# Two residual additions and a half moved onto TensorE at the end of four attention layers, one last store in place of two, and a new instruction order

## The chip, the cores and the metric

The kernel runs on one core of one Trainium2 chip. The metric is device time in microseconds (us) for one execution, taken as the median of several runs. The engines of the core are named as the profile names them: PE is TensorE (matrix products; PEld is its weight load), DVE is VectorE, ACT is ScalarE, POOL is GpSimd, SP is SyncE, which here only issues DMAs.

## The reference

One sequence of 2048 rows and 512 columns passes through four layers, each with layernorm in front and a residual around it:

```python
x = x + _A_ref(_layernorm(x), A_wqkv, A_wo)   # layer 1: linear attention
x = x + _B_ref(_layernorm(x), B_wqkv, B_wo)   # layer 2: sliding window of 256
x = x + _A_ref(_layernorm(x), A_wqkv, A_wo)   # layer 3, weights as layer 1
x = x + _B_ref(_layernorm(x), B_wqkv, B_wo)   # layer 4, weights as layer 2
```

Both kinds have 32 heads of 16. `_A_ref` maps queries and keys by phi (t + 1 above zero, exp(t) below), sums keys by values over the whole sequence and divides by a sum. `_B_ref` takes a masked softmax over the last 256 rows. Both end in a product with the 512 x 512 matrix `wo`; what comes out of it is added to x. The change touches that addition, in layer 4 alone.

## The kernel before, in words

Rows are worked in 16 tiles of 128. The residual stream x stays on the chip as `xres[:, t, :]`, in bfloat16. Layers are fused across the sequence: keys of layer 1, then its outputs with layer 2 tile by tile, then a barrier (layer 3 needs the sum over all tiles), then layer 3's outputs with layer 4.

A tile of layer 4 goes as follows. Scores are products on PE (L676, at the window's far edge L792 and L745), exponents of them on ACT (L686, L801, L754), masks on DVE (L694, L773) or POOL (L772). The products of weights and values run on PE (L822); DVE takes reciprocals (L834) and divides (L835) into `o`. `o` is transposed, by a DMA on SP (L389) or for the last tiles by PE with an identity (L395, L860) and a copy out (L402, L407). Then `tok` (L409 to L423) makes four products of 512 columns with `wBo` into one PSUM bank, in two groups of two (L420). `resid` (L602) lets DVE add the bank and `xres` into `xres` (L604, called `res`), and a store of 128 KB, `outp` (L942), goes out on POOL's or SP's queue.

The last tile has a function of its own, `b_last` (L849). It transposes and multiplies in halves as they become ready: a group of two products of 512 columns (L871), then two groups of two products of 256 columns. Two DVE additions of 256 columns follow (L877), each with a store of 64 KB on SP (L878).

`WHOLE` (L218) names tiles whose residual is to be added on PE, by a product of `ident` and `xres` into the same bank. It is empty for both layers, so that code lies idle.

Nothing is scheduled at run time. `Graph.add` collects operations with their readers and writers. All operations that touch one PSUM tile are chained: each depends on the one before it on that tile (`deps.add(last)`), whatever its columns. `place` unpacks `TABLE`, which holds for each operation its place in one overall order, its engine where it may have two (copies: ACT or DVE; far masks `mf`: DVE or POOL; `outp`: POOL or SP), and the PSUM bank of each tile. Each engine then plays its own operations strictly in that order and waits on semaphores where an input comes from another. A DMA waits in SP's line until its input is ready, and what stands behind it waits too.

The functions that the diff touches:

Of the kernel before, what the change touches and what calls it, by code (L numbers as in the profile page):

```python
# [9 lines left out]
ALU = mybir.AluOpType  # L10
# [207 lines left out]
WHOLE = {2: (), 3: ()}  # L218
# [17 lines left out]
class Plan:  # L236
# [173 lines left out]
    def tok(self, name, t, lhs, rhs, rd, key, whole=False):  # L410

        K = self
        ps = Tile(1, K.cls)
        if whole:
            self.pe("id", lambda e: e.matmul(K.ps(ps), K.ident[:], K.xres[:, t, :], start=True, stop=False), key - 0.01, 1, 512, rd=[("xres", t), ("ident",)], ps=[ps])
        for h in range(2):
            def put(e, h=h):
                m = None
                for c in (2 * h, 2 * h + 1):
                    m = e.matmul(K.ps(ps), lhs(c), rhs(c), start=c == 0 and not whole, stop=c == 3)  # L420
                return m
            self.pe(name, put, key - 0.001 * h, 2, 512, rd=rd, ps=[ps])
        return ps  # L423
# [170 lines left out]
    def a_out(self, t, key, whole):  # L594
        K = self
        x = lambda f: K.XQ[:, f, t * P:(t + 1) * P]
        po = self.tok("aout", t, x, lambda f: K.M[:, f, :], [("XQ", t)] + [("M", f) for f in range(4)], key + 0.1, whole)
        if whole:
            return po
        self.resid(t, po, key + 0.15)  # L600

    def resid(self, t, po, key):  # L602
        K = self
        self.on("DVE", "res", lambda e: e.tensor_tensor(K.xres[:, t, :], K.ps(po), K.xres[:, t, :], ALU.add), key, dve(512), rd=[("xres", t)], wr=[("xres", t)], ps=[po])  # L604
# [235 lines left out]
    def b_out(self, j, key, by_pe, whole=False):  # L840
        K = self
        s = j % 2
        self.transpose("oT", lambda: K.o[:, s, :], lambda: K.oT[:, s, :, :], [("o", s, 0), ("o", s, 1)], [("oT", s)], key - 0.15, by_pe)
        po = self.tok("bout", j, lambda f: K.oT[:, s, f, :], lambda f: K.wBo[:, f, :], [("oT", s), ("wBo",)], key, whole)
        if whole:
            return po
        self.resid(j, po, key + 0.05)

    def b_last(self, j, key):  # L849
# [4 lines left out]
        for h in range(2):  # L854
# [10 lines left out]
            for n in range(2) if h else [None]:  # L865
                cs = slice(0, D) if n is None else slice(256 * n, 256 * n + 256)

                def put(e, h=h, cs=cs):
                    m = None
                    for f in (h, h + 2):  # L870
                        m = e.matmul(K.ps(po)[:, cs], K.oT[:, s, f, :], K.wBo[:, f, cs], start=f == 0, stop=f == 3, skip_group_check=True)  # L871
                    return m

                self.pe("bout", put, key + 0.1 * h + 0.01 * (n or 0), 2, cs.stop - cs.start, rd=[("oT", s, h), ("wBo",)], ps=[po])
        for n in range(2):
            cs = slice(256 * n, 256 * n + 256)
            self.on("DVE", "res", lambda e, cs=cs: e.tensor_tensor(K.xres[:, j, cs], K.ps(po)[:, cs], K.xres[:, j, cs], ALU.add), key + 0.2 + 0.1 * n, dve(256), rd=[("xres", j)], wr=[("xres", j, n)], ps=[po])  # L877
            self.on("SP", "out", lambda e, cs=cs: e.dma_start(K.out[0, j * P:(j + 1) * P, cs], K.xres[:, j, cs]), key + 0.3 + 0.1 * n, (520, 2400), rd=[("xres", j, n)])  # L878
# [5 lines left out]
    def middle(self, ph):  # L884
# [14 lines left out]
        def front(t):  # L899
            k = base + t  # L900
            po = self.a_out(t, k - par["k_ao"], t in WHOLE[ph])
# [53 lines left out]
    r"c-qZZ1GH_+j;*AUO4YS(+qP}nwr$(CZQHhO+h*^z&%Lkz@5lf8{~o>0SxP0TnVDHN_6n(#3ZYPu0>vt{(khG!tBeY#;;UdPxccG}D67J&gzBTqtRkpSE~5J8",  # L955
    r"5~(cegG;Qksun7VilmaNY^tS-tg@?Cs*n2YqNp6IwMwQYsGKUfimLi5QE62hl|uDX(NtR%N~Ke|RXdeZEmn<GdevXmRuk0{HA!Vqb<_a0O)XUeRbACyrBahs",
    r"V>L)^R~^(cHAU4^JJeJaL)BLuRT{NZEmtvBF_lrRP@U9ZwM)fPomF&oOYK&%RYR3Y4N<q%3Ds5IQA1TX6;}mT2I8o@s=Lag;;Cuso@$~}tCMP&y050IH|msX",
    r"sv4-_YKA(kR;rn5l{%y5s#)r+TCEDIE=r(>daH`7HEN#9t0F*8wMPX~7J8`>s)SmrMk)ur)hP8&1%ml1BJ5SURA4BhvcMd*PmNZIV1b&g_N(_QE38usRV4VJ",
    r"&Zz_HqlygYRdrPi8o&khKqZDKkOYduLv>L_g>2AFtyh=SBb84bRF72<$PQ0bP$&VHRSpOSC84>>2~X7+6&yaPr0`jdQ)5*rIHbO)WY7?j!&emzzNxAzI$Tj9",
    r"pftpQ{OXyC2?}CC1(ge&8n1Fg5S0Q7sXUMp@<J#`1^J+`Dg$L9HGEfPRT>xvjUXhHgE$aW6;S0N9aMnvPyi}H5!D!KLu_aYwP2A-3sqEps0c+>JE#FQVS}ou",  # L960
    r"+Cv?v3-zF!st+BY2^?0Pp@wP$9iauZg;vlKHmWYr3|hkx)d`wIcX+Ojs;{mGOn|O%OihI2YLlw0UZ_d1SzT2x)k4^!CPO8)2(GCq&<&=-3D~L@!*$gYrol;=",
    r"4mZ>$SOV45W>^X{;1mEXgPCwsAuNZvumUvnf_bnKN~&2<Ud@Lsa2RT-*{}e%!V#DQ+n_g`hNG|@*1{{*57xnP*a0_TJ?w;4&<A$GYUm5MU=5rBf{?fYUaPZk",
# [12 lines left out]
    r"RJx;kQv`}eS*Q;kr0BGr`cg!iK!<3Co<uWs49ZH8C??gUi8Poh(=1(!Vo_BBj!nC1IK`noRGW~i&=}G@g6a_QI2uWNX)GP3$<&W_P+b~D_2?M&r=2vOM$=tg",
    r"pL)`9x~CgZFN#aMs5;%(4XGNPq$zZYrqXG;N{4A0ouGI$ovzanvh4U81?50Imx6J8x<MD|3^k(56r3AV0y;~VC?TDrCUk{D@p-yQO(`^Apk{Q7!f-ea$+u}9",
    r"-J$S2pO_a=1b#%(I4m1pNYObbhu~bih=gPCVrovgc?K<^7POyc(qn2#`{)VHqL>_upHd=<&57w5wdFXxl<razT1K;}9p9%p^qgOC5WYtzxIG8vlN^y>aw3kz",
    r"uQ&<E<>wTcU-Jt}%**K%zoZrPfTD0zF2pM-9v9(N6rW$wYD&t5IUncc1iXe4@@vY^YbhB&q>H?cPICdy!=?BVC+9MJhA;CKF3knG92e!Qe3mP4F}}vdxjc8{",
    r"68wg{b45<UCAlp3;7**9yKp5=#g(};r{=d@g$Hp}e#alFC)eh|Tv@;8H2i_9=(Ie9KT%gs$5nMd?!`lS0Dq?5+@I6)0?xp1=q)YeMO=*+b4NbMHFzMO=MLP5",
    r"`|>cZ&cnGT&*2eVhv)G~uFDsAE|21GT#M`Rcb?B{*qL=)pVx9Aqf7%{!RxspFJUmN7|lvv%8j@&2R5U5H8<gRG=`UPP_u!@@<txV8F>?D;_<whC-6sJ&YAf-",  # L980
    r"Pvjux22bKGJejlcR(?;}ISU6fH+dVkHrx3V@8DbfnQ!w>Zpt}$3h(0Ge24Gy9&W~ac`AS5544Z(aaL~5t@u9g=V{!UAMkW;!!7tBx8wtSlxOfUKFG&;CLiKi",
    r"e3&2cY(Bz|`3ZmJr~Hhy$!qc$GQ|v=BBr=0V2YZ2Cb%hR#N;<6j4_2wX%oVfG+|9)Q_6%hWlUMq)>sqXv@_*QdDG9dHxW!s6U&4&9ZX~s%5*dpOn=kKgf>x3",
    r"L^HrlFrCeE)5Q!lUCl((%?vV;%nCEugfYF$BooyPF%`{F6U}rtlT91b+r&0g%p$YW^fANCRMW#$GQ-VcGtKlhqs?@)#Pl>{%qla(EHh(GWfRAYFssc>Q_YMw",
    r"Ys^Sf#mq9}Om#ELR5i0rTvNleGWSd^Gshe?_f1W6+(eVL=7EVW$ILpj*Tj(ZX0F+19-4WkoWzv<W~n)2qMPzE-<&l&%p+4l7MPvpu{mcJnlEOTd1Bt1Z|14_",
    r"U}BhOW`l_(73HgmEeFj<v(dznJ?5~fZQ_~TCa%Oco6I4T*nBdTB#Egk@g#vcVy>8^riwf_2~8q%&1^PX%z1ObTs1GuEA!H9HA<41<bsmiY%>?kMRUV!H?Ivy",
    r"3b|xHo6F{ed1F$Fm6OIv9dpW@Ht{8p)HOFv5J@24O)yDow4{=BCZPlsl6QvXtx0dvNN}kyM$$<JlSo7|n#7V;s!AA1BGsgUgp*sQq1-lMCA9>W406YWkn1L+",
# [182 lines left out]
```

## Time and profile before

| what | us |
|---|---|
| median of 3 runs | 412.12 |
| lowest and highest run | 411.43 and 413.2 |
| the profiled execution, its own time | 412.6 |
| its span, first to last instruction | 410.8 |
| PE busy in the span | 386.9 |
| ACT busy | 352.8 |
| DVE busy | 344.5 |
| POOL busy | 122.4 |

The profiled execution lies 0.48 above the median, and 1.8 of its time lies outside the span. A line such as L604 is a line of the kernel's file. "x4" counts instructions. An entry in square brackets is the time in which the engine sat idle ahead of that instruction, and what ended the wait. A landing time runs from the issue of a DMA to its completion. The timeline merges neighbours on one line, so a row of x2 spans both.

### The profile page before, as it was taken

How to read it: one execution, taken by the hardware profiler on the slowest of the kernel's cores; microseconds unless marked ns; L12 is line 12 of the kernel's file. 1: busy time of each engine (PE TensorE's matmuls, PEld its weight loads, DVE VectorE, ACT ScalarE, POOL GpSimd, SP SyncE). 2: the span in 40 equal slices, each digit the busy share in tenths (PEclk: the TensorE clock that was granted, in tenths of full speed). 3: DMA queues.
4: the chain of work that ended last, by engine and by line, in shares of the span. 5: the costliest groups of instructions: out<-in, count | busy, mean ns of one | idle time of the engine just before them, and what ended most of it. 6: DMA issues, size and time to landing. Idle time of an engine off the chain costs nothing.

```text
span 410.8 us, 17540 instructions
## 1 busy us (share of the span) xinstructions
PE 386.9 (94%) x7668; PEld 260.3 (63%) x7742; DVE 344.5 (84%) x807; ACT 352.8 (86%) x448; POOL 122.4 (30%) x216
## 2 busy tenths in 40 slices
PE   7999999999999999999999999999999988999896
PEld 3654676766575576566567777586757755566674
DVE  6997799989998899888887789997899688857585
ACT  4654659998999999999998357999999999999993
POOL 4576653111252331320503203303113304303020
PEclk9999999999999999999999999999999999999999
DMA  7495114443243435353222100344314821561751
GB/s 249 101 217 144 49 34 115 120 70 90 56 106 74 119 77 107 81 119 82 68 41 57 27 2 2 105 109 81 102 44 122 122 66 41 120 127 56 168 107 42
DMA packets 66596, 37.19 MB, mean 91 GB/s; under 512 B 47640, under 2 KB 61848, under 8 KB 66520
## 3 DMA queue, kind: packets, MB, share of 16 engines
q1 hardware_dynamic: 66032, 34.75, 37.0%
q8 instruction: 61, 1.00, 1.1%
q0 software_dynamic: 480, 1.31, 1.0%
q14 instruction: 15, 0.12, 0.1%
q10 hardware_dynamic: 8, 0.00, 0.0%
HBM read 6.29 MB, written 2.10 MB: 20 GB/s over the span
## 4 chain that ended last, share of the span: by engine, by line
PE 51%; ACT 34%; DVE 9%; DMA 3%; issue 2%; SPq 1%; POOL 1%
ACT pb L686 20%; PE ps L420 18%; PE ps L434 10%; PE ps L822 10%; PE ps L676 5%; ACT pb L801 5%; ACT vp L686 4%; PE ps L501 3%; ACT tE L444 2%; DMA wA<-in_A_wqkv_dram 2%; DMA xT<-xn 1%; DVE xres L604 1%; DVE stats L374 1%; ACT pb L721 1%; PE ps L477 1%
## 5 line engine op out<-in xcount | busy, mean ns | idle before, releaser
L686 ACT ACTIVATE pb<-ps 128x1024 bf16<-128x1024 f32 (+2 forms) x216 | 198.9, 1020 | 5.2 <-PE ps L676 3.9
L822 PEld LDWEIGHTS ps<-vB,pb 128*128 128x128 bf16 x2560 | 77.7, 96 | 12.3 <-DVE pb L694 3.6
L822 PE MATMUL ps<-vB,pb 128*128 128x34 bf16 x2560 | 83.5, 177 | 0.6 <-POOL pb L772 0.3
L434 PE MATMUL ps<-xT,wBp 128*128 128x128 bf16 x1024 | 69.0, 219 | 1.7 <-ACT tE L444 0.6
L434 PEld LDWEIGHTS ps<-xT,wBp 128*128 128x128 bf16 x1024 | 58.5, 98 | 13.7 <-issue 4.4
L379 POOL TENSOR_SCALAR ve<-mv 128x1 f32<-128x1 f32 x63 | 16.7, 265 | 154.7 <-DVE mv L375 152.7
L444 ACT ACTIVATE tE<-ps 128x512 bf16<-128x512 f32 x64 | 38.6, 612 | 27.1 <-PE ps L420 11.2
L772 POOL TENSOR_SCALAR_AFFINE_SELECT pb<-pb 128x1024 bf16<-128x1024 bf16 x30 | 34.4, 1146 | 71.4 <-DVE pb L694 23.8
L676 PE MATMUL ps<-XQ,kB 32*128 32x256 bf16 (+3 forms) x992 | 48.0, 267 | 3.3 <-ACT pb L754 0.7
L604 DVE TENSOR_TENSOR xres<-ps,xres 128x512 bf16<-128x512 f32 x63 | 43.0, 684 | 6.7 <-PE ps L420 6.3
L420 PE MATMUL ps<-wA,XQ 128*128 128x512 bf16 x174 | 45.6, 379 | 2.2 <-issue 0.6
L374 DVE BATCH_NORM_STATS2 stats<-xres 128x6 f32<-128x512 bf16 x64 | 43.5, 685 | 2.8 <-DMA xres<-in_A_x_dram 2.2
L694 DVE TENSOR_TENSOR pb<-pb,tri 128x512 bf16<-128x512 bf16 (+1 forms) x108 | 41.5, 396 | 3.3 <-ACT pb L686 3.1
L801 ACT ACTIVATE pb<-ps 128x1024 bf16<-128x1024 f32 x42 | 41.4, 1059 | 1.1 <-PE ps L792 0.9
L380 POOL TENSOR_TENSOR rs<-ve,negh 128x1 f32<-128x1 f32 x64 | 37.8, 591 | 8.3 <-DVE ve L377 3.0
L434 PE MATMUL ps<-XQ,wA 128*128 128x128 bf16 x512 | 35.4, 219 | 0.3 <-DMA wA<-in_A_wqkv_dram 0.3
L434 PEld LDWEIGHTS ps<-XQ,wA 128*128 128x128 bf16 x512 | 30.7, 98 | 7.3 <-DMA wA<-in_A_wqkv_dram 0.8
L420 PE MATMUL ps<-wBv,xT 128*128 128x512 bf16 x110 | 31.4, 380 | 2.6 <-issue 1.0
L676 PEld LDWEIGHTS ps<-XQ,kB 32*128 32x128 bf16 x992 | 15.0, 92 | 29.5 <-ACT pb L686 7.5
L420 PE MATMUL ps<-M,XQ 128*128 128x512 bf16 x113 | 30.7, 380 | 2.3 <-ACT vp L686 0.4
L420 PE MATMUL ps<-wBo,oT 128*128 128x512 bf16 x105 | 28.8, 380 | 2.8 <-issue 1.0
L686 ACT ACTIVATE vp<-ps 128x1024 bf16<-128x1024 f32 (+2 forms) x32 | 26.7, 928 | 1.5 <-PE ps L676 1.5
(126 smaller groups left out, 551.6 us busy)
## 6 DMA issues: line engine op xcount, KB each, us to landing
vB<-vS SPq DMA_DIRECT2D x64, 136.0 KB, 2.7
kB<-vp SPq DMA_DIRECT2D x60, 128.0 KB, 2.3
wA<-in_A_wqkv_dram SPq DMA_DIRECT2D x3, 512.0 KB, 5.5
out_dram<-xres POOLq DMA_DIRECT2D x10, 128.0 KB, 2.8
xres<-in_A_x_dram SPq DMA_DIRECT2D x2, 512.0 KB, 5.1
pb<-in_B_wqkv_dram SPq DMA_DIRECT2D x1, 1024.0 KB, 5.8
xres<-in_A_x_dram SPq DMA_DIRECT2D x3, 256.0 KB, 5.5
out_dram<-xres SPq DMA_DIRECT2D x5, 128.0 KB, 2.7
```

The costliest lines, as they stand in the source:

```text
L374: self.on("DVE", "stats", lambda e: e.bn_stats(K.stats[:, t, :], x()), key, dve(512), rd=rd, wr=[("stats", t)], **held)
L380: self.pow = self.on("POOL", "pow", lambda e: e.tensor_tensor(K.rs[:, t, :], K.ve[:, t, :], K.negh[:], ALU.pow), key + 0.03, (640, 690), r ...
L420: m = e.matmul(K.ps(ps), lhs(c), rhs(c), start=c == 0 and not whole, stop=c == 3)
L434: m = e.matmul(K.ps(ps)[:, f * P:(f + 1) * P], w(c, f), xT(c), start=c == 0, stop=c == 3)
L444: self.on("ACT", "E", lambda e: e.activation(K.tE[:, s, :], K.ps(ps), ACT.Exp, bias=0.0), key, act(512), wr=[("tE", s)], ps=[ps])
L604: self.on("DVE", "res", lambda e: e.tensor_tensor(K.xres[:, t, :], K.ps(po), K.xres[:, t, :], ALU.add), key, dve(512), rd=[("xres", t)], w ...
L676: m = e.matmul(K.ps(ps[gq])[:, ns * i:ns * i + ns], K.kB[rows, j % 4, 2 * f + b, :, :], K.XQ[rows, f, q:q + ns], start=True, stop=True, ti ...
L686: return e.activation(out(2 * h, 2, ns), i, ACT.Exp, bias=0.0, scale=0.25)
L694: return e.tensor_tensor(x, x, K.tri[:, 0, sh:64].unsqueeze(1).unsqueeze(1).to_broadcast([P, 4, n, 64 - sh]), ALU.mult)
L772: return e.affine_select(out=x, in_=x, compare_op=ALU.is_ge, fill=0.0, base=-2, pattern=[[0, 16], [-2, 64]], channel_multiplier=1)
L801: return e.activation(far(h), i, ACT.Exp, bias=0.0, scale=0.25)
L822: m = e.matmul(K.ps(ps)[:, 34 * u:34 * u + 34], K.P((b // 2) % rp)[:, gq, f, o:o + P], K.vB[:, (b // 2) % 4, b % 2, r, :], start=i == 0, s ...
```

## The change

For tiles 13 and 14 of layer 4 a fifth product, identity by `xres`, closes the group in `tok`. The bank then holds the finished sum, and a copy (`rs`, on ACT or DVE) replaces the addition on DVE. For tile 15 the same is done for columns 256 to 511 alone: an identity product of 256 columns joins the first group; DVE adds columns 0 to 255 and a copy moves the rest. One store of 128 KB replaces the two of 64 KB and depends on both. `a_out` loses the argument `whole`, which it was never given as true.

```diff
-WHOLE = {2: (), 3: ()}
+WHOLE = {2: (), 3: (13, 14)}
...
-        if whole:
-            self.pe("id", lambda e: e.matmul(K.ps(ps), K.ident[:], K.xres[:, t, :], start=True, stop=False), key - 0.01, 1, 512, rd=[("xres", t), ("ident",)], ps=[ps])
         for h in range(2):
             def put(e, h=h):
                 m = None
                 for c in (2 * h, 2 * h + 1):
-                    m = e.matmul(K.ps(ps), lhs(c), rhs(c), start=c == 0 and not whole, stop=c == 3)
+                    m = e.matmul(K.ps(ps), lhs(c), rhs(c), start=c == 0, stop=c == 3 and not whole)
+                if whole and h:
+                    m = e.matmul(K.ps(ps), K.ident[:], K.xres[:, t, :], start=False, stop=True)
                 return m
...
+    def resid(self, t, po, key, whole=False):
+        K = self
         if whole:
-            return po
...
+            self.copy("rs", po, lambda: K.xres[:, t, :], lambda: K.ps(po), key, 512, wr=[("xres", t)])
+            return
...
                     for f in (h, h + 2):
                         m = e.matmul(K.ps(po)[:, cs], K.oT[:, s, f, :], K.wBo[:, f, cs], start=f == 0, stop=f == 3, skip_group_check=True)
+                    if not h:
+                        m = e.matmul(K.ps(po)[:, 256:512], K.ident[:], K.xres[:, j, 256:512], start=False, stop=False, skip_group_check=True)
...
-        for n in range(2):
-            cs = slice(256 * n, 256 * n + 256)
-            self.on("DVE", "res", lambda e, cs=cs: e.tensor_tensor(K.xres[:, j, cs], K.ps(po)[:, cs], K.xres[:, j, cs], ALU.add), key + 0.2 + 0.1 * n, dve(256), rd=[("xres", j)], wr=[("xres", j, n)], ps=[po])
-            self.on("SP", "out", lambda e, cs=cs: e.dma_start(K.out[0, j * P:(j + 1) * P, cs], K.xres[:, j, cs]), key + 0.3 + 0.1 * n, (520, 2400), rd=[("xres", j, n)])
...
+        self.on("DVE", "res", lambda e: e.tensor_tensor(K.xres[:, j, 0:256], K.ps(po)[:, 0:256], K.xres[:, j, 0:256], ALU.add), key + 0.2, dve(256), rd=[("xres", j)], wr=[("xres", j, 0)], ps=[po])
+        self.copy("rs", po, lambda: K.xres[:, j, 256:512], lambda: K.ps(po)[:, 256:512], key + 0.3, 256, rd=[("xres", j)], wr=[("xres", j, 1)])
+        self.on("SP", "out", lambda e: e.dma_start(K.out[0, j * P:(j + 1) * P, :], K.xres[:, j, :]), key + 0.4, (520, 2400), rd=[("xres", j, 0), ("xres", j, 1)])
```

`TABLE` is new as a whole. Unpacked and laid beside the old one it holds 2558 operations for 2559, and differs over the entire kernel, not at its end alone:

- Of the groups of PE 727 of 866 keep their relative order; of ACT's operations 394 of the 437 that it has in both tables, of DVE's 523 of 781, of SP's 137 of 225, of POOL's 135 of 197. In layers 2 to 4 most moves on PE and ACT are swaps of neighbours.
- 52 operations change engines: 24 far masks (14 to POOL, 10 to DVE), 7 `outp` (5 to SP, 2 to POOL), 21 copies (three of them in the place of DVE's additions). 346 of 1005 PSUM tiles get another bank.
- At the end: the copies of tiles 13 and 14 and the half of tile 15 stand on ACT; the copy that empties tile 15's second pair of transposes goes from ACT to DVE; tile 14's last products stand around, not behind, the first transposes of tile 15.
- At the start SP's order was x loads, transposes of tiles 5, 6, 7, a weight load of 1 MB (`wBn`), more transposes, and `wAv` (512 KB) after them all. It becomes transposes of tile 5, `wAv`, tile 6, `wAo` (512 KB), tile 7, `wBn`, the other transposes.
- Around the start of layer 4, ACT hands DVE the copies `bke` of tiles 1, 3 and 4 and the copy of one transposed tile (`Te`); DVE hands ACT `bve` of tiles 0 and 3, `bqe` of tile 4 and one copy `sc`.

More of the change, by code (lines that the diff above doesn't have):

```diff
@@ L419, in put @@
                 for c in (2 * h, 2 * h + 1):
-                    m = e.matmul(K.ps(ps), lhs(c), rhs(c), start=c == 0 and not whole, stop=c == 3)
-                return m
-            self.pe(name, put, key - 0.001 * h, 2, 512, rd=rd, ps=[ps])
+                    m = e.matmul(K.ps(ps), lhs(c), rhs(c), start=c == 0, stop=c == 3 and not whole)
+                if whole and h:
+                    m = e.matmul(K.ps(ps), K.ident[:], K.xres[:, t, :], start=False, stop=True)
+                return m
+            if whole and h:
+                self.pe(name + "i", put, key - 0.001 * h, 3, 512, rd=rd + [("xres", t), ("ident",)], ps=[ps])
+            else:
+                self.pe(name, put, key - 0.001 * h, 2, 512, rd=rd, ps=[ps])
         return ps
@@ L591, in barrier, with a_out @@
                 self.on("DVE", "pqd", lambda e, x=x, b=bc[tg]: e.tensor_tensor(x(), K.ps(b).rearrange("p (f n) -> p f n", f=4), x(), ALU.mult), k + 0.3 + 0.01 * tg, dve(512), rd=[("XQ", t)], wr=[("XQ", t)], ps=[bc[tg]])
-    def a_out(self, t, key, whole):
+    def a_out(self, t, key):
         K = self
         x = lambda f: K.XQ[:, f, t * P:(t + 1) * P]
-        po = self.tok("aout", t, x, lambda f: K.M[:, f, :], [("XQ", t)] + [("M", f) for f in range(4)], key + 0.1, whole)
+        po = self.tok("aout", t, x, lambda f: K.M[:, f, :], [("XQ", t)] + [("M", f) for f in range(4)], key + 0.1)
+        self.resid(t, po, key + 0.15)
+    def resid(self, t, po, key, whole=False):
+        K = self
         if whole:
-            return po
-        self.resid(t, po, key + 0.15)
-    def resid(self, t, po, key):
-        K = self
+            self.copy("rs", po, lambda: K.xres[:, t, :], lambda: K.ps(po), key, 512, wr=[("xres", t)])
+            return
         self.on("DVE", "res", lambda e: e.tensor_tensor(K.xres[:, t, :], K.ps(po), K.xres[:, t, :], ALU.add), key, dve(512), rd=[("xres", t)], wr=[("xres", t)], ps=[po])
@@ L871, in put @@
                         m = e.matmul(K.ps(po)[:, cs], K.oT[:, s, f, :], K.wBo[:, f, cs], start=f == 0, stop=f == 3, skip_group_check=True)
-                    return m
-                self.pe("bout", put, key + 0.1 * h + 0.01 * (n or 0), 2, cs.stop - cs.start, rd=[("oT", s, h), ("wBo",)], ps=[po])
-        for n in range(2):
-            cs = slice(256 * n, 256 * n + 256)
-            self.on("DVE", "res", lambda e, cs=cs: e.tensor_tensor(K.xres[:, j, cs], K.ps(po)[:, cs], K.xres[:, j, cs], ALU.add), key + 0.2 + 0.1 * n, dve(256), rd=[("xres", j)], wr=[("xres", j, n)], ps=[po])
-            self.on("SP", "out", lambda e, cs=cs: e.dma_start(K.out[0, j * P:(j + 1) * P, cs], K.xres[:, j, cs]), key + 0.3 + 0.1 * n, (520, 2400), rd=[("xres", j, n)])
+                    if not h:
+                        m = e.matmul(K.ps(po)[:, 256:512], K.ident[:], K.xres[:, j, 256:512], start=False, stop=False, skip_group_check=True)
+                    return m
+                if h:
+                    self.pe("bout", put, key + 0.1 * h + 0.01 * (n or 0), 2, cs.stop - cs.start, rd=[("oT", s, h), ("wBo",)], ps=[po])
+                else:
+                    self.pe("boutj", put, key, 3, 512, rd=[("oT", s, h), ("wBo",), ("xres", j), ("ident",)], ps=[po])
+        self.on("DVE", "res", lambda e: e.tensor_tensor(K.xres[:, j, 0:256], K.ps(po)[:, 0:256], K.xres[:, j, 0:256], ALU.add), key + 0.2, dve(256), rd=[("xres", j)], wr=[("xres", j, 0)], ps=[po])
+        self.copy("rs", po, lambda: K.xres[:, j, 256:512], lambda: K.ps(po)[:, 256:512], key + 0.3, 256, rd=[("xres", j)], wr=[("xres", j, 1)])
+        self.on("SP", "out", lambda e: e.dma_start(K.out[0, j * P:(j + 1) * P, :], K.xres[:, j, :]), key + 0.4, (520, 2400), rd=[("xres", j, 0), ("xres", j, 1)])
     def phase(self, ph):
@@ L959 @@
[L959 to L962, printed above, removed]
@@ L1007 @@
[L1007 to L1008 removed]
+    r"c-qZa1Gp?nvd#=;=Cy6xwr$(CZQHhO+qP}n=IiP+cXxINJ2P+geJ}fTR%K+wAAg|ot3JV$QlS*65Q>ymtU@bPVN_TZUx^B*tV*Cls_-hI%B()R;Oc{Gp(3b6",
+    r">b=XNBC1cWrOK)jt0XFt%BGU4Rw}!StR|>rs<n!ua;xNOqH3cisT?Y*N}<}SKFX-Hs-2pwVyZl9ipr__s>N!mN~ij%yegL3rfRF$YKd|xn(D8<x<+cLO0Nc}",
+    r"#ww1AtCp$lDy6EUim6m;hZ?Brs`hHR+NnCI3@V;lp^B?+YLMEc>Z$JPmg=aYt0t<x8mt1TPHKocp?0fjYN)!c66xuxsY<OntH7#(%BW_j7;2cxq`Ih?s)x#=",
@@ L1009 @@
+    r"jkW*hfJf5@<k4b-J{2#k+Dl7-Yx0zo=h)u^UP}aU_c`;FwfK4>pi?-Yxc)48I)**66p#deeLXA)$b~Nk-`8Ji@CxXe2egH+2mP7$Lj?30`x;&Q+l~C>JqSN>",
+    r"e@lAi9tS@OKan3!Rlo|A@yhEDQhW@&i@)q%oBX4c{=|DB`8&nu$vewDCjmv{fQQA4Un#G&-kSKQ`e}c0wFmD{pFa=khb?++f6AV>={NK}kt}{<<W1g|0gWQs",
+    r"_h8fi0Kou42m",
 )
```

104 lines of the change are left out of this document (50 added, 54 removed).

## The prediction

> **What bounds the kernel now.** I read the share of each engine on the page, then busy time by stretches, then the chain of work and the timelines of the last 12 us. The stretches:
>
> ```profile
> 9.79:44.00 34.21, 33.47 (x295) 18.98 (x304) 29.33 (x81) 17.91 (x32) 22.34 (x47) 1.00 0.62 156
> 60.00:247.00 187.00, 179.24 (x3604) 121.44 (x3642) 163.42 (x379) 168.40 (x208) 48.15 (x80) 1.00 0.35 79
> 247.00:259.00 12.00, 11.84 (x191) 8.99 (x193) 11.83 (x29) 9.87 (x19) 4.98 (x10) 1.00 0.12 36
> 259.00:292.00 33.00, 32.22 (x647) 22.63 (x652) 29.27 (x67) 33.00 (x39) 7.41 (x12) 1.00 0.38 86
> 292.00:324.00 32.00, 30.50 (x707) 21.45 (x708) 27.90 (x65) 31.52 (x36) 8.85 (x13) 1.00 0.48 97
> 324.00:395.00 71.00, 64.46 (x1708) 44.20 (x1716) 52.07 (x122) 69.62 (x82) 14.00 (x22) 1.00 0.44 97
> 395.00:407.20 12.20, 11.79 (x270) 7.84 (x270) 8.45 (x22) 8.40 (x16) 2.89 (x4) 1.00 0.33 81
> ```
>
> Columns are the stretch, its length, busy time of PE, PEld, DVE, ACT and POOL (instructions in brackets), the granted clock, the DMA share and GB/s. Layer 1 (9.79 to 44) is PE's: 33.47 of 34.21. PE and DVE share 247 to 259. ACT holds 259 to 395, with 1.86 idle of 136. In the 12 us before the closing additions PE is the full one again (11.79 of 12.20), while DVE and ACT work 70% of the time. The granted clock is 1.00 throughout. So DVE, which the change relieves, is not what the end waits for. The chain says it piece by piece (start, length, piece):
>
> ```profile
> 401.26 0.81 PE ps L420 x3
> ...
> 405.14 0.81 PE ps L420 x3
> 405.95 0.11 PE ps L860 x2
> 406.06 0.43 PE ps L871 x2
> 406.50 0.04 issue
> 406.54 0.62 PE ps L871 x4
> 407.16 0.02 issue
> 407.19 0.44 DVE xres L877
> 407.62 0.02 issue
> 407.65 0.42 DVE xres L877
> ```
>
> At 401.26 and 405.14 stand tile 13's and tile 14's products with `wBo`, behind each of which the change puts a fifth. At 406.06 and 406.54 stand tile 15's. DVE enters only at 407.19.
>
> **The change part by part: the end.** (a) Identity products. Four products of 512 columns without a gap took 0.86, one 0.215:
>
> ```profile
> 14.02 0.86 PE ps L501 x4
> ```
>
> Two of 512 columns and one of 256 (half, by columns) make 0.22 + 0.22 + 0.11 = 0.55, and they stand on the chain. Only a wait of PE could cover them, and the chain above shows none over 0.04; that one, ahead of 406.54, goes. That a transpose now stands between tile 14's products changes no sum. I take 0.5; the bounds are 0 (waits hide all) and 0.55.
>
> (b) The additions of tiles 13 and 14 leave DVE, copies come to ACT.
>
> ```profile
> L604 DVE TENSOR_TENSOR xres<-ps,xres 128x512 bf16<-128x512 f32 x63 | 43.0, 684 | 6.7 <-PE ps L420 6.3
> L407 ACT ACTIVATE XQ<-ps 128x512 bf16<-128x512 f32 x9 | 5.4, 605 | 0.6 <-PE ps L434 0.6
> ```
> ```profile
> 403.21 0.60 ACT L402 ACTIVATE oT<-ps 128x512 bf16<-128x512 bf16 x1 [0.25 <-PE ps L395]
> 405.00 0.26 DVE L834 RECIPROCAL rc<-ps 128x16 f32<-128x16 f32 x1 [0.36 <-PE ps L822]
> ```
>
> Each addition took 0.684 (second number behind the bar, in ns), and DVE soon idled after each: 0.36 ahead of the reciprocal at 405.00, 0.5 ahead of the closing pair (row under d). Their going gains nothing. On ACT the copy of tile 13, 0.605, stands ahead of the copy of tile 14's transposes at 403.21 and shifts its end from 403.81 to about 404.5. Tile 14's products want it at 405.14, so it is hidden: 0, and 0.6 if that cover were gone. The last copy of transposes moves from ACT to DVE, which has nothing else to do then: 0.
>
> (c) A far mask of 0.77 now stands in DVE's line ahead of the reciprocal of tile 14 and of two masks on which tile 15's first values wait.
>
> ```profile
> L773 DVE TENSOR_TENSOR pb<-pb,tri 128x1024 bf16<-128x1024 bf16 x20 | 15.2, 766 | 0.1
> ```
> ```profile
> 400.67 0.43 DVE L694 TENSOR_TENSOR vp<-vp,tri 128x512 bf16<-128x512 bf16 x1 [0.49 <-ACT vp L686]
> 401.24 0.26 DVE L834 RECIPROCAL rc<-ps 128x16 f32<-128x16 f32 x1
> ```
>
> DVE's idle time there swallows 0.49, and the gap from 401.10 to 401.24 another 0.14: 0.77 - 0.63 = 0.14. I take 0.1; bounds 0 and 0.77.
>
> (d) The closing pair. Addition and copy look parallel, one on DVE and one on ACT. But they read one PSUM tile, so `Graph.add` chains them, and ACT waits for DVE.
>
> ```profile
> L686 ACT ACTIVATE vp<-ps 128x256 bf16<-128x256 f32 x4 | 1.3, 381 | 0.7 <-PE ps L676 0.7
> L877 DVE TENSOR_TENSOR xres<-ps,xres 128x256 bf16<-128x256 f32 x2 | 0.8, 424 | 0.5 <-PE ps L871 0.5
> ```
>
> The old pair runs from 407.19 to 408.07, 0.88. The new one is 0.42 + 0.02 + 0.38 = 0.82. That makes -0.05. Side by side it would be -0.43, the lower bound; the upper is 0.
>
> (e) The last store. Before, half of it went out after the first addition, and only the second 64 KB were waited for. The rows are issues in three windows, 407.5 to 408, 404 to 406, and 396 to 404; the last number is us to landing.
>
> ```profile
> out_dram<-xres SPq DMA_DIRECT2D x1, 64.0 KB, 1.6
> ...
> out_dram<-xres SPq DMA_DIRECT2D x1, 128.0 KB, 2.1
> ...
> out_dram<-xres SPq DMA_DIRECT2D x1, 128.0 KB, 3.5
> ```
>
> 64 KB took 1.6; 128 KB took 2.1 in a quiet stretch and 3.5 in a crowded one. The end is quiet, so 2.1 - 1.6 = +0.5; bounds 0 and 1.9. The issue that is saved lay beside the second addition: 0.
>
> Here a page of the Trainium skill differs ("DMA: Bandwidth & Descriptors", section "Anatomy of one DMA — SWDGE (gpsimd) path"). It states a fixed cost near 2.0 us and bytes over 436 GB/s beside it. An estimate from that page: 64 KB more cost 0.15 us, and the sum would be 0.35 lower. The 1.6 of the first row is below its fixed part, and the page speaks of DMAs from POOL; the rows decide.
>
> The end together: 0.5 + 0 + 0.1 - 0.05 + 0.5 = **+1.05**.
>
> **The new order elsewhere.** After 259, where ACT is full, it loses `bke` twice and gains `bve` once and `bqe` once (0.605, above).
>
> ```profile
> L627 ACT ACTIVATE vp<-ps 128x512 bf16<-128x512 f32 x7 | 5.4, 777 | 0.7 <-PE ps L434 0.6
> L407 ACT ACTIVATE vS<-ps 128x512 bf16<-128x512 f32 x6 | 4.3, 712 | 0.0
> ```
>
> 0.71 + 0.61 - 1.55 = -0.23, say -0.25; bounds -0.25 and 0. Between 247 and 259 DVE takes two copies and gives two away: 0. Four far masks more on POOL relieve DVE where it bounds nothing: 0. SP takes three stores more of its own, and its line has idle time: 0.
>
> What the reshuffle does to waits no row gives. It can't gain more than the idle time of the full engines, 187.00 - 179.24 = 7.8 on PE in 60 to 247 and 1.86 on ACT in 259 to 395. It can lose wherever a DMA comes late in SP's line; one that did cost 2.4 (under R2). PE's and ACT's orders in layers 2 to 4 differ by swaps of neighbours, so I take 0.
>
> Sum: 1.05 - 0.25 = +0.8. The profiled execution, 412.6, would become 413.4. It lies 0.48 above the median of the runs shown; applied to that, 412.12 + 0.8 = **412.9**.
>
> **Rivals.** R1, faster: the new order closes waits in the long stretches. For it: 7.8 + 1.9 of idle time in small pieces, and the lines of DVE and SP, which release PE and ACT, changed most. Against it: PE and ACT play almost the same lines. A third of that time, 3.2, gives 412.9 - 3.2 = 409.7.
>
> R2, slower: weight loads ahead of transposes in layer 1. Transposes issued from 16.5 to 18.8 and from 20.5 to 22.8 (after the 1 MB load), and a piece of the chain:
>
> ```profile
> XQ<-vp SPq DMA_TRANSPOSE x2, 2.5
> ...
> XQ<-vp SPq DMA_TRANSPOSE x2, 4.8
> ...
> 318.42 4.92 DMA xT<-xn
> ```
>
> Behind the load a transpose took 4.8 instead of 2.5. Now 512 KB stand ahead of tile 6's and of tile 7's as well. PE idles 0.74 in that stretch, so what comes late there is paid: 4.8 - 2.5 = 2.3, about what the late one at 318.42 cost (4.92 - 2.5 = 2.4). It decides once tile 6's transpose lands over 2.6 after tile 5's, since six groups of two products, 0.43 each, stand between their uses. Against it: DVE prepares tile 5 earlier than before. 412.9 + 2.3 = 415.2. The Trainium skill's same page (section "Queues, rings and completion order") has descriptors consumed in ring order on each DMA engine, from which that delay would follow; 4.8 against 2.5 agrees.
>
> R3, the end does what it is built for: products, mask and store hide, addition and copy run side by side. Then -0.43 - 0.25 = -0.7: 411.4. Against it: PE's unbroken chain and `Graph.add`.
>
> **How the numbers follow.** Forecast 0.50, R1 0.18, R2 0.22, R3 0.10. A measurement of this kernel can tell about 0.5%, 2.06 us, from no change: 410.06 to 414.18. Forecast and R3 lie inside: same 0.60, faster 0.18, slower 0.22. The range reaches from R1's price to R2's, 409.7 to 415.2, and holds forecast and R3 (0.60) and about half of R1 and R2 (0.20). The bounds of the end without those that need a lost cover (-0.43 to +2.4: 0.55 + 1.9) give 411.4 to 414.5 and lie in it.
>
> **What would show it.** Right: from the first products of tile 13 to PE's last the path is longer by about 0.5; ACT's closing copy starts after DVE's addition has ended; the last store lands about 2.1 after its issue; the stretches before 395 shift by under 0.5. Wrong: copy and addition overlapping; a landing of 1.6; PE idle for over 1 us more between 10 and 44 (R2); PE's or ACT's long stretches shorter by over 1 (R1). If the stretches before 395 together move by over 2 either way, the forecast falls, whatever the end does.

## The result, and the profile after

| what | before | after |
|---|---|---|
| median of 12 runs each, us | 412.65 | 415.25 |
| lowest and highest run | 411.43 and 413.76 | 412.22 and 417.77 |
| the profiled execution, its own time | 412.6 | 414.65 |
| its span | 410.8 | 412.9 |
| from its start to PE's last product's end | 407.16 | 409.42 |

The ratio is 1.0064, interval 1.0037 to 1.0091: slower by 0.6%, and 0.05 above the top of the range. Measured once more beside the later experiments (run e11 below) the same kernel had a median of 413.86, ratio 1.0040 (1.0018 to 1.0063). That is again slower, but inside the range: on which side of 415.2 the kernel falls changes from one measurement to the next, that it is slower does not. The runs of the kernel after spread over 5.5 us, those of before over 2.3. That spread is part of what has to be explained.

The stretches of the kernel after, in the columns of the prediction's first fence:

```profile
9.79:44.00 34.21, 33.82 (x299) 18.44 (x299) 30.05 (x80) 17.27 (x31) 22.45 (x44) 1.00 0.56 141
60.00:247.00 187.00, 183.76 (x3648) 121.91 (x3646) 163.94 (x377) 168.22 (x207) 50.59 (x82) 1.00 0.38 81
...
259.00:292.00 33.00, 31.45 (x621) 21.37 (x610) 27.65 (x63) 31.55 (x38) 8.09 (x14) 1.00 0.39 92
...
395.00:407.20 12.20, 11.26 (x307) 8.29 (x304) 8.42 (x22) 9.63 (x17) 0.00 (x0) 1.00 0.58 105
```

Layer 1 is full on PE (33.82 of 34.21), so rival R2's late transposes did not come: tile 6's landed at 17.36, 1.7 after tile 5's and not over 2.6. Two rows changed for the worse: from 259 to 292 ACT, which was busy all 33.00, now has 1.45 idle, and from 395 to 407.2 PE has 0.94 idle against 0.41. The clock is 1.00 as before. To place these losses I compared the start of each exponent on ACT (an operation that both kernels have, at the same place of the computation) in the two traces. The offset is within 0.3 of zero just ahead of 282 and +1.7 behind it; some 0.7 is given back by 330; it is +1.5 by 393, and +2.0 at 398.64 of before. So nearly the whole loss of 2.15 stands before the end that the change rebuilds.

**The step at 282.** ACT's row, before and then after:

```profile
281.91 3.78 ACT L686 ACTIVATE pb<-ps 128x1024 bf16<-128x1024 f32 x4
```
```profile
283.62 1.94 ACT L690 ACTIVATE pb<-ps 128x1024 bf16<-128x1024 f32 x2 [1.34 <-PE ps L680]
```

ACT waits 1.34 for scores, the products in front of the exponents. Followed back in the timelines of PE and DVE of the kernel after:

```profile
283.17 0.40 PE L680 MATMUL ps<-XQ,kB 32*128 32x256 bf16 x8 [1.51 <-DVE vS L407]
...
281.81 0.73 DVE L632 CAST vp<-ps 128x512 bf16<-128x512 f32 x1 [1.69 <-PE ps L418]
282.44 0.67 DVE L407 CAST vS<-ps 128x512 bf16<-128x512 f32 x1
```

PE waits for DVE, and DVE stood idle 1.69 ahead of L632, the evacuation `bke` of tile 5's keys. That copy writes a staging room of which there are two, by `room = self.room[st]` with `st = t % 2`. Tile 5 gets the room of tile 3, which two key DMAs (`kd`, L640) must first have read. In the table as unpacked, the second of tile 3's stands later in SP's line than before. SP's timeline, before and after:

```profile
271.73 1.14 SPq L636 DMA_DIRECT2D kB<-vp  x2
```
```profile
272.39 0.59 SPq L640 DMA_DIRECT2D kB<-vp  x1
273.03 0.62 SPq L659 DMA_DIRECT2D vB<-vS  x1
273.75 2.50 SPq L389 DMA_TRANSPOSE xT<-xn  x1
276.29 1.27 SPq L389 DMA_TRANSPOSE oT<-o  x1
277.61 1.23 SPq L640 DMA_DIRECT2D kB<-vp  x2
```

Before, the pair is issued at 271.73. After, the pair is torn apart: its second half, the first of the row of x2, is issued at 277.61, behind a transposition of `xn` and one of `o`. The DMA view of 277.5 to 277.9 gives its landing (last number):

```profile
kB<-vp SPq DMA_DIRECT2D x1, 128.0 KB, 4.1
```

277.61 + 4.1 = 281.7, and DVE starts at 281.81. The bracket names PE as the releaser; by these times it was the DMA. The trace also holds the instruction in which DVE waits for the semaphores of tile 3's two key DMAs: it ends at 281.77, 0.03 after the landing.

**The second loss.** SP's line and PE's near 396, before and after. The rows of the kernel before are one of each view, in two fences:

```profile
392.32 1.25 SPq L389 DMA_TRANSPOSE oT<-o  x1
```
```profile
396.67 1.04 PE L420 MATMUL ps<-wBo,oT 128*128 128x512 bf16 x4
```
```profile
393.02 1.19 SPq L659 DMA_DIRECT2D vB<-vS  x2
394.25 1.31 SPq L389 DMA_TRANSPOSE oT<-o  x1
```
```profile
398.78 1.04 PE L418 MATMUL ps<-wBo,oT 128*128 128x512 bf16 x4 [0.70 <-DMA oT<-o]
```

The transposition of tile 12's `o` stood ahead of one of tile 14's two value DMAs; now it stands behind both, and PE waits 0.70 for it.

**The end.** The chain of waits of the kernel after from tile 13's products on, then the last rows of ACT's and SP's timelines, then the landing of the last store:

```profile
403.02 0.97 PE ps L418 x4
403.99 0.21 PE ps L420
...
408.09 0.22 PE ps L420
...
408.85 0.11 PE ps L875
...
409.45 0.43 DVE xres L882
```
```profile
409.91 0.38 ACT L407 ACTIVATE xres<-ps 128x256 bf16<-128x256 f32 x1 [0.97 <-DVE xres L882]
```
```profile
410.32 0.33 SPq L884 DMA_DIRECT2D out_dram<-xres  x1
```
```profile
out_dram<-xres SPq DMA_DIRECT2D x1, 128.0 KB, 1.7
```

The three identity products (L420 twice, L875) stand on the chain with 0.21, 0.22 and 0.11. Copy and addition stand one behind the other, 409.45 to 410.29, 0.84 against 0.88. The 128 KB land in 1.7, hardly longer than the 64 KB in 1.6.

### The profile page after: what moved, and what is told of

The parts are those of the page before. It is cut to its first block, busy times and chain, and to the rows that moved or that the text cites. A ratio compares the mean times of both kernels' runs of the same rounds, so it can differ in the third digit from the quotient of the medians.

```text
span 412.9 us, 17627 instructions
## 1 busy us (share of the span) xinstructions
PE 396.5 (96%) x7745; PEld 261.6 (63%) x7745; DVE 343.2 (83%) x802; ACT 353.2 (86%) x449; POOL 125.3 (30%) x217
## 4 chain that ended last, share of the span: by engine, by line
PE 54%; ACT 23%; DVE 10%; DMA 3%; POOL 2%; issue 1%; SPq 0%; POOLq 0%
PE ps L418 18%; ACT pb L690 12%; PE ps L826 12%; PE ps L437 11%; PE ps L680 6%; ACT vp L690 4%; ACT pb L805 3%; DVE XQ L594 2%; PE ps L796 1%; PE ps L504 1%; DVE stats L374 1%; DMA oT<-o 1%; DVE xres L608 1%; DMA XQ<-xn 1%; PE ps L480 1%
## 5 line engine op out<-in xcount | busy, mean ns | idle before, releaser
L690 ACT ACTIVATE pb<-ps 128x1024 bf16<-128x1024 f32 (+2 forms) x216 | 198.6, 1020 | 7.5 <-PE ps L680 6.8
L826 PEld LDWEIGHTS ps<-vB,pb 128*128 128x128 bf16 x2560 | 78.6, 96 | 12.1 <-DVE pb L698 3.1
L776 POOL TENSOR_SCALAR_AFFINE_SELECT pb<-pb 128x1024 bf16<-128x1024 bf16 x35 | 40.1, 1145 | 70.2 <-DVE pb L698 29.3
L418 PE MATMUL ps<-wA,XQ 128*128 128x512 bf16 x192 | 49.6, 380 | 1.1 <-ACT pb L805 0.4
L608 DVE TENSOR_TENSOR xres<-ps,xres 128x512 bf16<-128x512 f32 x61 | 41.6, 684 | 7.9 <-PE ps L418 7.4
L418 PE MATMUL ps<-wBv,xT 128*128 128x512 bf16 x128 | 35.4, 381 | 0.2 <-ACT pb L690 0.2
L418 PE MATMUL ps<-wBo,oT 128*128 128x512 bf16 x124 | 33.3, 381 | 1.0 <-DMA oT<-o 0.7
L418 PE MATMUL ps<-M,XQ 128*128 128x512 bf16 x128 | 33.5, 380 | 0.6 <-ACT vp L690 0.4
L838 DVE RECIPROCAL rc<-ps 128x16 f32<-128x16 f32 x64 | 16.1, 252 | 16.3 <-PE ps L826 15.9
```

Source lines behind the costliest of these rows:

```text
L418: m = e.matmul(K.ps(ps), lhs(c), rhs(c), start=c == 0, stop=c == 3 and not whole)
L690: return e.activation(out(2 * h, 2, ns), i, ACT.Exp, bias=0.0, scale=0.25)
L776: return e.affine_select(out=x, in_=x, compare_op=ALU.is_ge, fill=0.0, base=-2, pattern=[[0, 16], [-2, 64]], channel_multiplier=1)
L826: m = e.matmul(K.ps(ps)[:, 34 * u:34 * u + 34], K.P((b // 2) % rp)[:, gq, f, o:o + P], K.vB[:, (b // 2) % 4, b % 2, r, :], start=i == 0, s ...
```

## The experiments

A theory and two rivals follow from this. **W**: a few DMAs that stand too late in SP's line cost the time, through the waits above; the end costs a few tenths. **E**: the rebuilt end costs it. **O**: the new lines of all engines cost it, in many places. Under W an order can be mended by moving a few DMAs; under O it can't so easily, and under E not at all. The recorded texts of e1 to e4 use the letter O for what is called W here. Each run is put against runs of the kernel before on the same chip.

### The end alone, the order alone

The first kernel has the changed code with the old table (copies of tiles 13, 14 and the half of 15 on ACT, the last copy of transposes on DVE). The second has the old code with the new table.

```diff
 e1_end_alone:   code of after
-TABLE of after
+TABLE of before, with the three copies and the single store in the places of what they replace
 e2_order_alone: code of before
-TABLE of before
+TABLE of after, with additions and two stores in the places of the copies and the one store
```

> The change's code with the order of before; only the three new copies go to ACT and the last copy of transposes to DVE, as in the changed kernel. Theory O (the loss sits in the new order, in two DMAs that stand later in SP's line): the end costs 0.5 for the identity products, -0.05 for the closing pair and 0.1 for the last store, so 0.55 over before, ratio 1.0013. Theory E (the loss is the end's, and what the order loses is given back by ACT's full stretch): 2.0 to 2.6 over before, ratio 1.005 to 1.006.

> The code of before with the order of the changed kernel; additions of tiles 13 and 14 on DVE and the last copy of transposes on ACT, as before. Theory O: 2.0 over before, ratio 1.005, with DVE idle for 1.7 ahead of a bke copy (L628) near 282 and PE waiting near 398 for a transpose. Theory E: 0 to 0.6 over before.

Measured: e1 413.14, ratio 1.0013 (1.0000 to 1.0026); e2 415.13, ratio 1.0057 (1.0032 to 1.0082). The order alone brings the loss and the spread (412.22 to 417.49 over e2's runs); the end alone costs about 0.5, as the first text had it. E falls.

A finer measure of the end comes from the traces. I take the start of one pair of exponents (L686 or L690, 128x256), ahead of all that the change touches at the end. These are ACT's rows in before, after, e1, e7 (told below) and e8 (below), one fence each:

```profile
398.64 0.66 ACT L686 ACTIVATE vp<-ps 128x256 bf16<-128x256 f32 x2
```
```profile
400.63 0.66 ACT L690 ACTIVATE vp<-ps 128x256 bf16<-128x256 f32 x2 [0.47 <-PE ps L680]
```
```profile
397.79 0.67 ACT L690 ACTIVATE vp<-ps 128x256 bf16<-128x256 f32 x2
```
```profile
398.43 0.67 ACT L688 ACTIVATE vp<-ps 128x256 bf16<-128x256 f32 x2
```
```profile
399.57 0.67 ACT L690 ACTIVATE vp<-ps 128x256 bf16<-128x256 f32 x2
```

From there to the last instruction (the spans are 410.77, 412.92, 410.25, 410.45 and 411.28) it takes 12.13 before, 12.29 after, 12.46 in e1, 12.02 in e7 and 11.71 in e8. The number is steady: the kernel after gave 12.29 and 12.30 in two executions, before and e9, which have the same end, 12.13 and 12.12. So the new end with its own order costs 0.16, and with the old order 0.33. The 0.16 holds a gain of the order too: the old end under the new order (e2, and e10 below) takes 12.06 and 11.99, so that under this order the new end costs 0.2 to 0.3.

### The two late DMAs brought forward

```diff
 e3: SP's line of after
 kd tile 3, first
+kd tile 3, second
 vd tile 2
 T tile 6
 oT tile 0
-kd tile 3, second
 e4: as e3, and
 vd tile 14 (first half)
+oT tile 12
 vd tile 14 (second half)
-oT tile 12
```

`kd` are key DMAs, `vd` value DMAs, `T` and `oT` the transpositions of `xn` and `o`.

> The changed kernel with one operation moved: the second DMA kd of tile 3 in layer 4 stands right behind the first in SP's line, ahead of two transposes. Theory O: DVE's wait of 1.7 ahead of the bke copy of tile 5 goes, and the kernel gets 1.0 to 1.5 faster than the changed one: 1.1 to 1.6 over before, ratio 1.003 to 1.004. Theory E: as the changed kernel, 1.006.

> As e3_kd_earlier, and the transpose of tile 12's o in layer 4 stands ahead of the second vd of tile 14 in SP's line, as in the order of before. Theory O: PE's wait near 398 shrinks by 0.6; 0.5 to 1.0 over before, ratio 1.001 to 1.0025. Theory E: as the changed kernel, 1.006.

Measured: e3 414.46, ratio 1.0046 (1.0029 to 1.0063); e4 413.16, ratio 1.0019 (1.0004 to 1.0033). In e3 the gap at 282 is gone and the wait for `oT` is still there, in ACT's and in PE's timeline:

```profile
283.56 3.78 ACT L690 ACTIVATE pb<-ps 128x1024 bf16<-128x1024 f32 x4
```
```profile
398.76 1.04 PE L418 MATMUL ps<-wBo,oT 128*128 128x512 bf16 x4 [0.99 <-DMA oT<-o]
```

But e3's time lies between what the text has for the two theories (1.004 and 1.006), and its profiled execution ends as late as that of after. The offset of the exponents is already +1.7 ahead of 282, where it was 0.3 in after, for PE waits for other transpositions. PE's waits from 138 to 165:

```profile
PE ps L437 <- DMA xT<-xn: 0.6, 1, 0.6
PE ps L418 <- DMA XQ<-xn: 0.5, 1, 0.5
```

In the profiled execution of e2, one of that kernel's slowest (417.49), the offset is +2.2 ahead of 282, and a further 1.9 comes near 370. So the places of the loss change from one execution to the next.

In e4, with both moved, two of the 230 operations in SP's line, the kernel lies where e1 lies (1.0019 against 1.0013). Its highest run is 415.18 instead of 417.77. That speaks for W. Against the second measurement of after (1.0040) the gain is within the noise.

### SP's line alone, and all the others alone

```diff
 e5: lines of PE, ACT, DVE, POOL as after
-SP's line as after
+SP's DMAs in the order of before, as far as their inputs allow
 e6: lines of PE, ACT, DVE, POOL as before
-SP's line as before
+SP's DMAs in the order of after, as far as their inputs allow
```

> The changed kernel with its new lines of PE, ACT, DVE and POOL, but SP's DMAs in the relative order of before. Theory S (of the new order it is SP's line alone that costs): what is left is the end, 0.5 to 0.8 over before, ratio 1.0013 to 1.002, and the spread of the runs shrinks from 5.5 to about 2.5. Rival theory X (the new lines of the engines cost by themselves, as they lean on PSUM banks and buffers differently): 1.5 to 2.6 over before, ratio 1.004 to 1.006.

> The kernel of before, unchanged but for SP's line, whose DMAs stand in the relative order of the changed kernel. Theory S: 1.5 to 2.5 over before, ratio 1.004 to 1.006, runs spread over 4 or more. Theory X: within 0.5 of before.

Measured: e5 422.48, ratio 1.0247 (1.0221 to 1.0272), in 6 runs; e6 433.5, ratio 1.0506 (1.0480 to 1.0532), in 5. Both expectations missed by far, under either theory. Neither line is bad in itself; what counts is that SP's fits the others'. The granted clock of both is lower as well (0.992 and 0.974 over the profiled executions, 1.00 in before), so a part of these two times may be the clock's. In e6 the step at 282 comes back, with DVE idle for 4.62 instead of 1.69, and every link can be read. SP's timeline, its wait, then DVE's timeline:

```profile
282.75 1.19 SPq L389 DMA_TRANSPOSE xT<-xn  x1
283.99 1.27 SPq L389 DMA_TRANSPOSE oT<-o  x1
285.30 1.23 SPq L636 DMA_DIRECT2D kB<-vp  x2
```
```profile
SPq L389 <- DVE xn L381: 7.0, 1, 7.0
```
```profile
282.32 0.41 DVE L381 TENSOR_SCALAR xn<-xres,mv,rs 128x512 bf16<-128x512 bf16 x1
287.35 0.73 DVE L628 CAST vp<-ps 128x512 bf16<-128x512 f32 x1 [4.62 <-DMA kB<-vp]
```

SP's line holds the transposition of tile 6 ahead of the key DMA, as after, but DVE's old line writes that `xn` only at 282.32. The transposition waits 7.0 at the head of SP's line, the key DMA behind it, ready since long, is issued at 285.30, and DVE, idle for 4.62, writes the room at 287.35. Here the bracket does name the DMA. In e5 the same happens elsewhere. SP's timeline and its wait:

```profile
208.38 0.56 SPq L659 DMA_DIRECT2D vB<-vS  x1
213.19 1.19 SPq L389 DMA_TRANSPOSE XQ<-xn  x1
214.43 1.42 SPq L659 DMA_DIRECT2D vB<-vS  x1
215.89 1.30 SPq L389 DMA_TRANSPOSE oT<-o  x1
```
```profile
SPq L389 <- DVE vp L407: 5.0, 1, 5.0
```

The first of these transpositions waits 5.0 for its input, the two DMAs behind it wait with it, and ACT's exponents lie 4.8 later behind this place than ahead of it.

### The parts of the end

e7 is e1 without the three identity products: the residual of tiles 13, 14 and of half of tile 15 is left out. e8 has the old order and the old additions for tiles 13 and 14, and gives tile 15's two halves a PSUM tile each, so that nothing chains the closing copy to the addition.

```diff
 e7
-                if whole and h:
-                    m = e.matmul(K.ps(ps), K.ident[:], K.xres[:, t, :], start=False, stop=True)
 ...
-                    if not h:
-                        m = e.matmul(K.ps(po)[:, 256:512], K.ident[:], K.xres[:, j, 256:512], start=False, stop=False, skip_group_check=True)
 e8
-WHOLE = {2: (), 3: (13, 14)}
+WHOLE = {2: (), 3: ()}
 ...
-        po = Tile(1, K.cls)
+        po, pr = Tile(1, K.cls), Tile(1, K.cls)
 ...
-                        m = e.matmul(K.ps(po)[:, 256:512], K.ident[:], K.xres[:, j, 256:512], start=False, stop=False, skip_group_check=True)
+                        m = e.matmul(K.ps(pr)[:, 256:512], K.ident[:], K.xres[:, j, 256:512], start=False, stop=False, skip_group_check=True)
 ...
-        self.copy("rs", po, lambda: K.xres[:, j, 256:512], lambda: K.ps(po)[:, 256:512], key + 0.3, 256, rd=[("xres", j)], wr=[("xres", j, 1)])
+        self.copy("rs", pr, lambda: K.xres[:, j, 256:512], lambda: K.ps(pr)[:, 256:512], key + 0.3, 256, rd=[("xres", j)], wr=[("xres", j, 1)])
```

> As e1_end_alone, but the three identity products are left out, so the residual of tiles 13 and 14 and of half of tile 15 is not added in layer 4. If the products stand on the path, 0.45 less than e1_end_alone: 0.1 to 0.2 over before, ratio 1.0003. If PE's waits hide them, as e1_end_alone, 1.0013.

> The order of before, tiles 13 and 14 added on DVE as before; only tile 15 is changed: its halves go to two PSUM banks, the second with an identity product of 256 columns, so that DVE's addition and ACT's copy need not wait for each other, and one store of 128 KB follows. If the chain through one bank is what keeps the close at 0.82, the close takes 0.45 now; with 0.11 for the product and 0.1 for the store that is 0.2 to 0.3 less than before, ratio 0.9993 to 0.9995. If not, 0.1 to 0.2 over before.

Measured: e7 412.26, ratio 0.9994 (0.9981 to 1.0007); e8 412.51, ratio 1.0002 (0.9986 to 1.0019). In time e7 lies 0.0019 of the ratio under e1, 0.8 us, with an uncertainty as large. In the traces it is 12.46 - 12.02 = 0.44: the identity products are paid almost in full. In e8 the closing pair overlaps. DVE's and ACT's timelines:

```profile
407.82 0.42 DVE L883 TENSOR_TENSOR xres<-ps,xres 128x256 bf16<-128x256 f32 x1 [0.29 <-PE ps L874]
```
```profile
408.03 0.38 ACT L407 ACTIVATE xres<-ps 128x256 bf16<-128x256 f32 x1 [0.70 <-PE ps L874]
```

ACT starts 0.21 after DVE and not after its end. That end is 0.42 shorter than the old one (11.71 against 12.13), a thousandth of the time, which the timed runs can't show. e8 is the best end found, but no kernel here was measurably faster than the kernel before.

### The reverse: the kernel before made late, the order mended, the change again

```diff
 e9: code and table of before, SP's line
 kd tile 3, first
-kd tile 3, second
 vd tile 2
 oT tile 0
 vd tile 3
 kd tile 4, kd tile 4
+kd tile 3, second
 ...
 vd tile 14
-oT tile 12
 vd tile 14
+oT tile 12
 e10: e2 (code of before, new order) with the two moves of e4
 e11: the kernel after, unchanged
```

The text of e9 says layer 3; the keys are those of the fourth layer. The text of e10 has `oT` of tile 12 ahead of both value DMAs of tile 14; as built it stands between them, as in e4.

> The kernel before, whole, with two DMAs later in SyncE's line and nothing else changed: the second key DMA of tile 3 (layer 3) behind the first vB DMA and the transposition and the two key DMAs that followed it, so that it is issued near 277.5 instead of near 272.3, as in the kernel after; and the transposition oT of tile 12 behind one more vB DMA, some 0.6 later. Theory W (the order's loss is the lateness of these two DMAs, by the wait that each sets): the evacuation of tile 5's keys on VectorE waits for the key DMA and ScalarE shows a gap of about 1.3 near 282, an offset of +1.4 behind it, of which up to half is given back by 330; PE waits 0.6 to 0.8 for oT<-o near 397; sum +1.4 to +2.0, so 413.5 to 414.1 against 412.1, ratio 1.0034 to 1.0049. Rival V (the two waits cost only in the company of the rest of the new order; in the old one other work is in hand): ratio below 1.0015, and no gap on ScalarE over 0.5 near 282.

> The kernel before with its old end (adds on VectorE, two stores) under the new orders of all engines, as in the second experiment, but with the two DMAs moved forward in SyncE's line: the second key DMA of tile 3 right behind the first, oT of tile 12 ahead of the two vB DMAs of tile 14. Theory W: the order costs nothing once these two are early, so 412.1 +- 0.5, ratio 0.999 to 1.0015. Rival V: the second experiment's other stalls (1.3 between 138 and 160, 1.1 near 365) belong to the order, and half or more of its +2.4 stays: ratio 1.003 to 1.006.

> The changed kernel itself, a second time, for its spread and for a second profiled execution. Theory W: the same two stalls (a gap of 1.0 or more on ScalarE near 282, PE waiting 0.6 or more for oT<-o near 398) and 414.5 to 415.5, ratio 1.005 to 1.008. Rival J (the loss is of stalls at changing places, other ones in each execution): neither stall at its place, a loss of the same size elsewhere.

Measured: e9 414.2, ratio 1.0039 (1.0013 to 1.0064); e10 413.06, ratio 1.0021 (1.0001 to 1.0041); e11 413.86, ratio 1.0040 (1.0018 to 1.0063). e9 falls into W's numbers. DVE's row and the landing of the DMAs issued from 278.6 to 279.4 read as after, and ACT waits 1.52 at 284.01. Here too DVE's semaphore wait ends 0.03 after the key DMA's landing (282.16 and 282.13):

```profile
282.20 0.72 DVE L628 CAST vp<-ps 128x512 bf16<-128x512 f32 x1 [1.89 <-PE ps L420]
```
```profile
kB<-vp SPq DMA_DIRECT2D x2, 128.0 KB, 3.6
```

But that is the key DMA alone: the late `oT` cost nothing in e9, for PE came to it late enough. The second of W's two terms is thus shown for the new order only. That the sum fits is in part luck. The step at 282 is 1.6, of which 0.7 is given back by 325, and the profiled execution has two further losses: PE waits 0.9 near 185 and 0.5 near 386 for transpositions that nobody moved. e10 lies between the two expectations (412.1 and 413.5 or more): the two moves take back 0.0036 of the order's 0.0057, with an uncertainty of about 0.003, and the interval leaves the rest open between nothing and 0.004. Its profile shows no wait of PE for a DMA over 0.5.

e11 lies below W's 414.5 to 415.5 and corrects it at one point. In this second profiled execution of the kernel after there is no gap at 282, although the key DMA was issued as late as in the first (277.97). DVE's row, and the landing of that DMA:

```profile
280.68 0.72 DVE L632 CAST vp<-ps 128x512 bf16<-128x512 f32 x1
```
```profile
kB<-vp SPq DMA_DIRECT2D x1, 128.0 KB, 2.0
```

It landed in 2.0 instead of 4.1, at 280.0, ahead of its use. In before it was issued at 272.3, landed 3.4 later at 275.7 and was wanted at 279.8: 4 us to spare. After, DVE comes to the room some 2.5 us after the issue (280.12 - 277.61), and what the landing takes beyond that DVE waits (4.1 - 2.5 = 1.6, idle 1.69). The wait for `oT` was there again:

```profile
397.84 1.04 PE L418 MATMUL ps<-wBo,oT 128*128 128x512 bf16 x4 [0.72 <-DMA oT<-o]
```

A third loss stood where the first execution had none, near 95: DVE waited for a key DMA on a room in layer 2. DVE's wait from 92 to 105:

```profile
DVE vp L632 <- DMA kB<-vp: 0.9, 1, 0.9
```

So the new order does not always stall at 282. The reading that fits these traces is that it has used up the slack of several DMAs, two of which the experiments moved, and that each execution pays where a landing is long. It fits the wider spread, which e2 shows and e1 does not (411.98 to 413.88). What makes one landing 2.0 and another 4.1 no run here shows.

## Why the prediction was wrong

**Right:** what bounds the kernel, and the end's mechanism. PE has no slack at the end, and identity products cost what they last: 0.44 of 0.55 in e1 against e7, predicted 0.5. From the first products of tile 13 to PE's last the path grew by 0.5 as forecast (403.02 to 409.42 is 6.40; 401.26 to 407.16 is 5.90). In the trace of before one of tile 13's four products has no record (x3 in the row of the chain); e9, which has the same end and all four, gives 5.96, so 0.45 is nearer. But tile 13's products start 0.2 earlier against the exponents in the new order, so that only 0.27 is left of it. The additions on DVE gained nothing by going. Addition and copy run one behind the other, as read from `Graph.add` (0.84; predicted 0.82), and e8 shows the other branch: in two tiles they overlap.

**Mis-sized, (e), the last store.** "The end is quiet, so 2.1 - 1.6 = +0.5" failed. It measured 1.7, so +0.1; from the closing pair's end to the last instruction it is 2.63 after (410.29 to 412.92) and 2.70 before (408.07 to 410.77). The 2.1 of a store three us earlier didn't hold for the last one. Here the estimate from the Trainium skill's page "DMA: Bandwidth & Descriptors", section "Anatomy of one DMA — SWDGE (gpsimd) path", 0.15 us for 64 KB more, was the nearer one, although its fixed 2.0 us is above both landings. With (a) and (c) at 0.27, the pair at -0.04 and the store at -0.07 the end costs 0.16 instead of 1.05.

**Failed, the step that decided:** "PE's and ACT's orders in layers 2 to 4 differ by swaps of neighbours, so I take 0." Those lines do differ little. SP's does not, and it was named a sentence earlier as the place where a loss can arise, then priced at nothing. SP's line was taken to have idle time and so to cost nothing; what decided was when single DMAs in it land. The order cost 2.0 in the first profiled execution (the offset at 398.64) and 1.05 in the second, 0.0057 of the time alone (e2). By the medians two of SP's 230 DMAs make most of it (e4 and e10, and e9 for the one); other DMAs without slack make the rest in some executions (e2, e3, e11). R2's 415.2 is the measured time but for 0.05, by luck: it has a late DMA of the right kind, but in layer 1, where nothing was lost (offset -0.1 at 63); the places were others, in layer 4 above all, and no single one cost 2.3 in the end. The gain of 0.25 on ACT after 259, from fewer copies there, can't be seen beside the stalls. R1 counted 7.8 of idle time on PE from 60 to 247 that could be won. Most of it is not idle time: before's trace has 3604 matmul records there and after's 3648, with which PE is busy for 183.76 of the 187 although at the end of that stretch the exponents are only 0.3 later.

The prediction's own test, that the forecast falls if the stretches before 395 move by over 2, came out at +1.5 there and 2.0 a few us later, and the smaller sign it named, a shift under 0.5, failed.

Open are the rest of 0.002 in e10 (nothing to 0.004), the share of each DMA, and what sets the landing times.

## What to carry to other kernels

When an instruction order is made anew, compare each in-order DMA line first: for every DMA that moved back, list what stands ahead of it, what each of those waits for, and which buffer its completion sets free; what comes late beyond the slack, the engine behind it waits for (here 1.6 by that sum, 1.69 measured), and the kernel loses that or a part of it. One DMA that empties a buffer, three places later, made DVE wait 1.69, more than the 0.44 of all the arithmetic that the change adds to PE; swaps of neighbours on PE and ACT were not tested alone. And when a kernel's runs spread more than before, look for slack that has been used up rather than for one fixed stall.

## What the runs showed that was not expected

- One key DMA of 128 KB, issued at the same place of the same kernel (277.61 and 277.97) behind the same transposition, took 4.1 us in one execution and 2.0 in another.
- SP's line and the other engines' lines, each from a kernel of 412 to 415 us, took 422.48 and 433.5 in the two mixtures: SP's order cost most here where it was made for other lines of the engines.
- A store of 128 KB at the very end landed in 1.7 to 1.8 us (after, e1, e8), one of 64 KB in 1.6.
- In e6 the granted clock was 0.83 to 0.85 in three of the seven stretches of 16 us from 288 to 400 (320 to 336, 368 to 384, 384 to 400), with PE busy for 11.88 to 13.07 of the 16, and 0.94 to 1.00 in the other four. In before it was 1.00 in all seven, with PE busy for 14.04 to 15.73. Whether the stalls brought the clock down no run shows.
- The releaser in brackets is the one that came last by the profile: in after and e9 it named PE where the key DMA, by its landing and by DVE's semaphore wait, was what DVE waited for; in e6, with a wait of 4.62, it named the DMA.
